# Where the forms of x and the sums of h are made: two layers of attention and squared-ReLU MLP, the MLP's first product by seven products

## The chip, the core and the metric

The kernel runs on one core of a Trainium2 chip. The metric is the time of one execution in device microseconds (us); each kernel is run several times and the median is given. The engines have the names of the profile: PE (matrix products; PEld is its loading of weights), DVE (vector engine), ACT (scalar engine), POOL (GpSimd) and SP, which here only issues transfers. Each engine executes its own instructions in the order in which they were written, and waits at an instruction until what it needs is there.

## The reference

Two layers, all in fp32, on x of 2048 rows and 640 columns: attention with 32 heads of 20, then an MLP with 1536 hidden columns.

```python
def _A_ref(x, wqkv, wo):
    q, k, v = ...                      # (x @ wqkv), 32 heads of 20
    scores = jnp.einsum("bhqd,bhkd->bhqk", q, k) * (Dh ** -0.5)
    p = _softmax(scores, axis=-1)
    o = jnp.einsum("bhqk,bhkd->bhqd", p, v)
    return o.transpose(0, 2, 1, 3).reshape(B, S, D) @ wo
def _B_ref(x, w1, b1, w2, b2):
    h = x @ w1 + b1
    h = jnp.where(h > 0, h, 0) ** 2
    return h @ w2 + b2
for _ in range(2):
    x = x + _A_ref(_layernorm(x), A_wqkv, A_wo)
    x = x + _B_ref(_layernorm(x), B_w1, B_b1, B_w2, B_b2)
```

## The kernel before

**Products in three terms.** PE multiplies in fp32r, a shorter form of fp32. Each operand is kept as two parts: `hi`, a cast to fp32r that ACT makes, and `lo = src - hi`, a subtraction, called lower part here. A product is three: hi hi, hi lo, lo hi (`THREE`).

**Stages of a layer.** Attention; then the *heads* (`add_heads`: the product with w_o, added to x, 32 half tiles of 128 x 320, four blocks of 512 rows in the order `HEADS = (1, 0, 2, 3)`, stored to `d_x`); then the MLP's first product (class `Up`) and its second product (class `Down`).

**First product.** It goes over four blocks of 512 rows in the order `UPS = (1, 2, 3, 0)`; a block has six units (`unit(qb, j, ...)`). The depth of 640 is five parts of 128. Four of them, as a 2 x 2 matrix of blocks, are multiplied by seven products instead of eight (Winograd's form of Strassen's scheme); the fifth is multiplied plainly. For this a unit needs *forms* of w_1 (A11, S2, S1, A22, S3, A12, S4; made once and kept in DRAM) and of x. Those of x are made anew for each block: `B11`, `B21`, `B22` are blocks of the normalised, transposed x, `T1_` to `T4_` are sums and differences of them, `LAST` is the fifth part and `LAST + 1` ("xd") a difference of it. A unit is 54 matmuls of 128 x 256 in the order A11, the product S4 of the unit before (its `tail`), S2, S1, A22, S3, A12, which use B11, B22, T2_, T1_, T4_, T3_ and B21. DVE adds the products out of the PSUM banks (L1498 `add(u1, bank[1], u0)`, L1523 to L1525 and L1546), ACT copies the first bank (L1493) and makes bias, ReLU and square. Units alternate between two sets of four banks, so PE can be a few products ahead of these sums and no more.

**Making the forms (class `Forms`).** For each half tile of rows (numbers 0 to 3 in a block; the second index of a form, 0 or 1, is the half of the rows):
- `load`: x from `d_x` to a tile (an SP transfer); `stats`: mean and variance (DVE L317, L318, then two small POOL instructions L320, L321); `turned`: normalise and transpose on DVE (L350, L355), store to `d_t`; `fetch`: four transfers that read it back across all partitions as `y`.
- `sums`, `third`, `fourth`: the sums T on POOL (`pool_lo`, L344).
- `split`, `plain`, `diff`: for a form, the cast on ACT (L460) and right behind it the lower part (L461) on DVE; only for T3_ and T4_ on POOL. `late` does this for B21, whose tile comes free with the block before.

**What sets the order.** `unit` calls `side()` seven times, 42 times in a block. Each call executes the entry of a table for that step: `Forms.PLACES[n]` for the next block and `Forms.PLACES[n - 42]` for the one after it (negative numbers are steps of the block before). The block that comes first is prepared beside the heads, by `BESIDE_HEADS`, one step for each of the 32 half tiles (`between`). SP issues all transfers in the order written, weights of w_1 and w_2 among them (`more`, `bring`).

**Sums of h for the second product.** `Down` uses seven products too (for all row blocks, but for the last block in layer 1). They need sums of four quarters of h. Before the change `tail` of a unit makes two of them on POOL when the unit's h is ready (L1551 and L1555, and a `pool_lo` behind each), stores one beside h (`d_h1`), and `Down.fetch` loads it again. `Down.make` makes the operands of a step of the second product two steps (`LEAD`) before its use.

Of the kernel before, what the change touches and what calls it, by code (L numbers as in the profile page):

```python
# [43 lines left out]
def tile_layers(  # L44
# [264 lines left out]
    d_h1 = dram.tile([NQB, NP, P, 2, P], F32, name="d_h1")  # L309
# [55 lines left out]
    class Forms:  # L365
# [3 lines left out]
            -9: [("load", 0), ("load", 2)],  # L369
            -3: [("stats", 0)],  # L370
            -1: [("stats", 2)],
            0: [("load", 1), ("load", 3)],
            3: [("turned", 0)],
            5: [("stats", 1)],
            9: [("turned", 2)],
            10: [("fetch", 0)],
            12: [("stats", 3)],
            16: [("turned", 1)],
            17: [("fetch", 2)],
            19: [("turned", 3)],  # L380
            21: [("sums", 0), ("third", 0)],
            23: [("split", B11, 0), ("fetch", 1)],
            24: [("split", B22, 0)],
            25: [("plain", 0)],
            26: [("split", T1_, 0)],
            27: [("split", T2_, 0), ("fetch", 3)],
            28: [("fourth", 0)],
            30: [("split", T3_, 0)],
            31: [("split", T4_, 0), ("diff", 0)],
            32: [("split", B11, 1)],  # L390
            33: [("split", B22, 1)],
            34: [("plain", 1)],
            35: [("sums", 1), ("third", 1)],
            37: [("split", T1_, 1)],
            38: [("split", T2_, 1)],
            40: [("split", T3_, 1), ("fourth", 1)],
            41: [("split", T4_, 1), ("diff", 1)],
        }
        BESIDE_HEADS = {
            10: [("load", 0), ("load", 2)],  # L400
            12: [("stats", 0)],
            13: [("stats", 2)],
            14: [("turned", 0)],
            15: [("turned", 2), ("load", 1), ("load", 3)],
            17: [("fetch", 0), ("stats", 1)],
            18: [("fetch", 2), ("stats", 3)],
            19: [("turned", 1)],
            20: [("turned", 3)],
            21: [("sums", 0)],
# [45 lines left out]
        def into(self, dst, src, i, lo=nc.vector.tensor_sub):  # L455
            hi_, lo_ = (
                dst[:, h, :, i * P : (i + 1) * P].rearrange("p k (a i) -> p k a i", a=4)
                for h in range(2)
            )
            nc.scalar.copy(hi_, src)  # L460
            lo(lo_, src, hi_.bitcast(F32))  # L461

# [1489 lines left out]
```

## Time and profile before

| what | value |
|---|---|
| median of 3 runs | 3566.66 us (3566.16 to 3568.74) |
| the profiled execution | 3570.83 us, span of its trace 3569.1 us |
| PE busy | 3511.4 us, 98% of the span |
| DVE, ACT, POOL busy | 2787.7, 2837.6 and 973.1 us (78%, 80%, 27%) |
| heads, layer 1 and 2 | about 1376 to 1444 and 3155 to 3224 us of the span |
| first product | 1449.2 to 1636.2 and 3227.9 to 3417.2 us |
| second product | 1636.2 to about 1747 and 3417.2 to about 3560 us |

The rest is attention. The profile gives for each engine when it was busy, and for each rest of an engine which instruction or transfer ended it. A busy PE can still be slow: the granted clock beside it says at which share of its full speed it ran. Line numbers in the rows are those of the kernel before (after the change the same lines stand up to 16 further on or 1 or 2 back).

### The profile page before, as it was taken

The numbers are of one execution on the slowest core, as the hardware profiler recorded it, in microseconds if no ns is written. First come the engines' busy times: TensorE is split into PE (matmuls) and PEld (weight loads), VectorE is DVE, ScalarE is ACT, GpSimd is POOL, SyncE is SP. The second block draws the span as 40 slices with busy tenths as digits, with TensorE's granted clock in tenths as the row PEclk, the third lists the DMA queues.
The fourth block names the chain that finished last, engine by engine and source line by source line (L and its number), as shares of the span: only waits on it lengthen the run. The fifth ranks groups of instructions, "written<-read, shape, count | busy, mean of one in ns | idle before, by whom it ended". The sixth has DMA issues, their size and how long they took to land.

```text
span 3569.1 us, 74141 instructions
## 1 busy us (share of the span) xinstructions
PE 3511.4 (98%) x26404; PEld 2167.9 (61%) x26404; DVE 2787.7 (78%) x5512; ACT 2837.6 (80%) x5038; POOL 973.1 (27%) x1213
## 2 busy tenths in 40 slices
PE   9999999999999999899999999999999999998899
PEld 8998333333333337889989973333333333378899
DVE  8999888888888872656869988888888888636567
ACT  5889999999999993354348899999999999934543
POOL 4430345444422121431143201212121212114410
PEclk9999999999999999999999999999999999999999
DMA  7666445444322137755666652222222121377554
GB/s 258 228 211 180 140 138 153 121 123 146 113 66 60 51 107 263 240 197 195 234 195 223 196 169 69 76 79 57 70 82 57 44 58 51 112 267 241 202 197 145
DMA packets 325056, 518.72 MB, mean 145 GB/s; under 512 B 74836, under 2 KB 149588, under 8 KB 324688
## 3 DMA queue, kind: packets, MB, share of 16 engines
q1 hardware_dynamic: 324160, 512.29, 45.8%
q8 instruction: 209, 3.42, 0.4%
q10 hardware_dynamic: 528, 1.70, 0.2%
q14 instruction: 159, 1.30, 0.1%
HBM read 331.14 MB, written 182.69 MB: 144 GB/s over the span
## 4 chain that ended last, share of the span: by engine, by line
PE 88%; DMA 4%; DVE 2%; issue 2%; ACT 2%; POOL 1%; SPq 1%; DVEq 0%; POOLq 0%; ACTq 0%
PE banks L946 27%; PE banks L931 18%; PE banks L837 17%; PE banks L1658 8%; PE banks L532 5%; PE banks L544 5%; PE banks L1463 4%; PE banks L512 2%; DMA y<-d_t 1%; SPq L80 1%; DVE xf L461 1%; DMA x<-d_x 1%; PE banks L527 1%; DMA d_t<-x 0%; PE banks L644 0%
## 5 line engine op out<-in xcount | busy, mean ns | idle before, releaser
L941 ACT ACTIVATE e<-banks 128x512 f32<-128x512 f32 (+1 forms) x3416 | 2035.3, 692 | 56.4 <-PE banks L931 20.9
L848 DVE TENSOR_REDUCE mx<-banks 128x1 f32<-128x512 f32 x2560 | 1619.5, 684 | 322.9 <-PE banks L837 271.6
L946 PE MATMUL banks<-e,vg 128*32 128x512 f32 x8192 | 1093.5, 605 | 2.3 <-ACT e L941 2.1
L837 PE MATMUL banks<-k,q 60*128 60x512 f32 x3360 | 1062.2, 411 | 0.7 <-DMA d_qk<-ev 0.7
L931 PE MATMUL banks<-q,k 62*128 62x512 f32 x4096 | 1049.6, 441 | 1.3 <-ACT v L608 0.6
L931 PEld LDWEIGHTS banks<-q,k 62*128 62x128 f32 x4096 | 514.9, 184 | 748.6 <-ACT e L941 441.4
L837 PEld LDWEIGHTS banks<-k,q 60*128 60x128 f32 x3360 | 569.8, 185 | 196.3 <-ACT e L941 63.6
L877 DVE CUSTOM_DVE_ANT_0 rl<-banks,rl 128x512 f32<-128x512 f32 x736 | 476.8, 688 | 31.4 <-PE banks L837 6.9
L870 ACT ACTIVATE rl<-banks 128x512 f32<-128x512 f32 x736 | 399.6, 602 | 56.8 <-PE banks L837 46.9
L946 PEld LDWEIGHTS banks<-e,vg 128*32 128x32 f32 x8192 | 162.2, 108 | 352.8 <-issue 268.6
L1463 PE MATMUL banks<-xf,w 128*128 128x256 f32 x2448 | 327.3, 293 | 46.5 <-DVE r L1524 16.3
L1463 PEld LDWEIGHTS banks<-xf,w 128*128 128x128 f32 x2448 | 313.4, 200 | 57.3 <-DVE r L1524 19.7
L544 PE MATMUL banks<-xnT,wqk 64*128 64x512 f32 x1080 | 327.6, 393 | 0.0
L532 PE MATMUL banks<-xnT,wqk 64*128 64x512 f32 x1080 | 327.1, 395 | 0.0
L990 POOL TENSOR_TENSOR few<-few,minus_t 128x16 f32<-128x16 f32 x62 | 179.9, 2901 | 243.8 <-DMA few<-d_s 243.7
L1001 POOL TENSOR_TENSOR o<-o 128x512 f32<-128x512 f32 x62 | 79.6, 1283 | 500.6 <-DMA o<-d_r 261.2
L341 POOL CAST mr<-nt 128x32 fp32r<-128x32 f32 x64 | 13.4, 209 | 742.2 <-DVE nt L903 742.2
L837 PE MATMUL banks<-kd,q 60*128 60x512 f32 x736 | 212.5, 398 | 0.8 <-ACT rl L870 0.6
L544 PEld LDWEIGHTS banks<-xnT,wqk 64*128 64x128 f32 x1080 | 202.1, 188 | 7.9
L532 PEld LDWEIGHTS banks<-xnT,wqk 64*128 64x128 f32 x1080 | 200.0, 187 | 11.1 <-issue 1.7
L532 PE MATMUL banks<-wv,xnT 64*128 64x320 f32 x960 | 193.5, 308 | 0.0
L544 PE MATMUL banks<-wv,xnT 64*128 64x320 f32 x960 | 190.4, 306 | 0.0
(150 smaller groups left out, 3543.1 us busy)
## 6 DMA issues: line engine op xcount, KB each, us to landing
q<-d_qk SPq DMA_DIRECT2D x876, 80.0 KB
d_qk<-ev SPq DMA_DIRECT2D x80, 512.0 KB
k<-d_qk SPq DMA_DIRECT2D x444, 80.0 KB
x<-d_x SPq DMA_DIRECT2D x96, 320.0 KB
w<-d_w SPq DMA_DIRECT2D x60, 480.0 KB
w<-d_w SPq DMA_DIRECT2D x48, 512.0 KB
d_o<-ot SPq DMA_DIRECT2D x248, 80.0 KB
ot<-d_o SPq DMA_DIRECT2D x38, 512.0 KB
```

What stands on the lines that cost most here:

```text
L532: top = nc.tensor.matmul(dst, a[:64], b[:64], start=start, stop=last)
L544: low = nc.tensor.matmul(dst, a, b, start=False, stop=last, skip_group_check=True)
L837: nc.tensor.matmul(dst, q_t[t][b : b + 60, p, sub * P : (sub + 1) * P], k_t[t // NQB, c][b : b + 60, p, :], start=True, stop=True,)
L848: nc.vector.tensor_reduce(maxima(t)[:, 2 * p + par, sub, c : c + 1], dst, axis=AX.X, op=ALU.max)
L870: nc.scalar.activation(r, dst, AF.Relu)
L877: nc.vector.tensor_tensor_reduce(out=r[par], in0=dst, in1=r[par], scale=1.0, scalar=LEAST, op0=ALU.add, op1=ALU.max, accum_out=maxima(t)[: ...
L931: nc.tensor.matmul(dst, k_t[t // NQB, kt // 4][b : b + 62, p, (kt % 4) * P : (kt % 4 + 1) * P], q_t[t][b : b + 62, p, :], start=True, stop ...
L941: nc.scalar.activation(dst, src, AF.Exp, scale=SCALE)
L946: nc.tensor.matmul(acc[32 * h : 32 * h + 32, :], v_t[t // NQB, kt // 8][:, kt % 8, 32 * h : 32 * h + 32], es[p][:, par, :], start=(kt == 0 ...
L990: nc.gpsimd.tensor_tensor(few, few, minus_t, op=ALU.pow)
L1463: nc.tensor.matmul(dst, w, v, start=n == 0 and not more, stop=n == len(todo) - 1, skip_group_check=more,)
L1658: nc.tensor.matmul(dst, a, b, start=first and not more, stop=last, skip_group_check=more)
```

## The change

The forms of x are made at other places and partly on another engine, and so are the sums of h:
- `cast` (ACT) and `low` (the lower part, now always on POOL) are separate entries of the tables, so that several casts can stand ahead of several lower parts. `both` does one and then the other. `late` makes both casts of B21 and then both lower parts, at step 0 of its block rather than 2.
- Both tables are new. Beside the heads the forms of the first block are made at steps 2 to 26 rather than 10 to 29, and from the tiles that `add_heads` has just made (`done`), so that these four tiles are not loaded from `d_x`. The first loads for the next block leave at step 26 of the heads rather than 29.
- The sums of h leave `Up`. `Down.sums` makes them on POOL in the second product, one step ahead of `make`; `d_h1` with its 30 stores and 30 loads is gone.
- The first three slots of w_1 are loaded in the last block of attention into tiles of k that are no longer used; beside the heads 12 slots are loaded instead of 14.

```diff
-            21: [("sums", 0), ("third", 0)],
-            23: [("split", B11, 0), ("fetch", 1)],
...
+            14: [("sums", 0), ("third", 0)],
+            15: [("cast", B11, 0), ("cast", B22, 0)],
+            16: [("turned", 3), ("low", B11, 0), ("low", B22, 0), ("cast", T2_, 0)],
...
-            24: [("split", T2_, 0), ("split", B21, 0)],
...
+            18: [("both", B11, 0), ("both", B22, 0), ("both", T2_, 0), ("both", T1_, 0)],
...
-    def into(self, dst, src, i, lo=nc.vector.tensor_sub):
...
-        nc.scalar.copy(hi_, src)
-        lo(lo_, src, hi_.bitcast(F32))
...
+        def cast(self, n, i):
+            self.part(n, i, lambda dst, src, i: nc.scalar.copy(self.at(dst, 0, i), src))
+        def low(self, n, i):
+            self.part(n, i, lambda dst, src, i: pool_lo(
+                self.at(dst, 1, i), src, self.at(dst, 0, i).bitcast(F32)
+            ))
...
+        for n, u in enumerate((6, 10, 14)):
+            def early(n=n):
...
+                del k_t[NG - 1, n]
+                kept.pop(((NG - 1) % 4, n))
+                w_1.load(n)
+            loads[t0 + 3, u] = early
...
+            if done is not None:
+                done[i] = x
...
-                if whole and pair:
-                    s = u0.rearrange("p (u c) -> p u c", u=2)
-                    nc.gpsimd.tensor_tensor(s, r[:, :, 2, :], r[:, :, 3, :], op=ALU.add)
-                    pool_lo(r[:, :, 2, :], r[:, :, 0, :], r[:, :, 2, :])
...
+        def sums(self, n):
+            un, grp, j = self.steps[n]
+            if grp:
+                return
+            raw = self.raw[un, j]
+            s = self.s[un, j] = xtile("s")[:, : 4 * P].rearrange("p (i f c) -> p f i c", f=2, i=2)
+            nc.gpsimd.tensor_tensor(s[:, 0], raw[:, :, 2, :], raw[:, :, 3, :], op=ALU.add)
+            pool_lo(raw[:, :, 2, :], raw[:, :, 0, :], raw[:, :, 2, :])
...
+                if n + self.LEAD + 1 < len(self.steps):
+                    self.sums(n + self.LEAD + 1)
...
-            made[UPS[1]].do(Forms.PLACES, {29: -9, 30: -3, 31: -1}.get(n))
-            more(n % 2 if n < 28 else 0)
+            made[UPS[1]].do(Forms.PLACES, {26: -12, 28: -8, 29: -5, 31: -1}.get(n))
+            more(n % 2 if n < 24 else 0)
...
-            add_heads(qb, x_a, x_m, xs, between)
+            add_heads(qb, x_a, x_m, xs, between, made[UPS[0]].x if n == 0 else None)
...
-                    if n == 2 and m:
+                    if n == 0 and m:
                         made[UPS[m]].late()
```

How the order of instructions moves is seen at three places of layer 1. A row is line, operation, output, inputs and size; the number behind a name tells tiles apart. DVE in the last unit of the first block, before: L1498, L1523 to L1525 and L1546 are the sums from the banks, `xf` and `xd` the lower parts of forms of the next block.

```order
L1498 TENSOR_TENSOR us_17129<-banks,us_17129 128x256
L461 TENSOR_TENSOR xf_17012<-t_17137,xf_17012 128x2x128
L461 TENSOR_TENSOR xf_17027<-t_17137,xf_17027 128x2x128
L317 BN_STATS bst_17182<-x_17109 128x6 x2
L318 BN_AGGR mv_17183<-bst_17182 128x2
L1523 TENSOR_TENSOR us_17129<-banks,us_17129 128x256
L1524 TENSOR_TENSOR r_17198<-banks,us_17129 128x2x128
L1525 TENSOR_TENSOR r_17198<-banks,us_17129 128x2x128
L461 TENSOR_TENSOR xd_17078<-t_17137,xd_17078 128x128
L317 BN_STATS bst_17223<-x_17111 128x6 x2
L318 BN_AGGR mv_17224<-bst_17223 128x2
L1546 TENSOR_TENSOR r_17198<-banks,us_17129 128x2x128
```

The same unit after the change; the sums are now L1514, L1538 to L1540 and L1561.

```order
L1514 TENSOR_TENSOR us_17121<-banks,us_17121 128x256
L316 BN_STATS bst_17153<-x_17066 128x6 x2
L317 BN_AGGR mv_17154<-bst_17153 128x2
L1538 TENSOR_TENSOR us_17121<-banks,us_17121 128x256
L1539 TENSOR_TENSOR r_17189<-banks,us_17121 128x2x128
L1540 TENSOR_TENSOR r_17189<-banks,us_17121 128x2x128
L349 TENSOR_SCALAR y_17206<-x_17064,mv_17115 128x5x4x32
L354 STREAM_TRANSPOSE x_17064<-y_17206 128x640
L1561 TENSOR_TENSOR r_17189<-banks,us_17121 128x2x128
```

Three lower parts are gone from between the sums; statistics have moved up, and normalising and transposing a tile of the block after the next (L349, L354) stands ahead of the last sum.

DVE at the end of the heads, before: L1443 is the add of a half tile, L317 and L318 are statistics of the first two tiles of the second block, L1498 is the first sum of the first product.

```order
L1443 TENSOR_TENSOR x_16375<-banks,x_16375 128x320
L461 TENSOR_TENSOR xd_16547<-t_16522,xd_16547 128x128
L1443 TENSOR_TENSOR x_16419<-banks,x_16419 128x320
L317 BN_STATS bst_16645<-x_16624 128x6 x2
L318 BN_AGGR mv_16646<-bst_16645 128x2
L1443 TENSOR_TENSOR x_16419<-banks,x_16419 128x320
L317 BN_STATS bst_16668<-x_16626 128x6 x2
L318 BN_AGGR mv_16669<-bst_16668 128x2
L1498 TENSOR_TENSOR us_16676<-banks,us_16676 128x256
```

After the change, with L1457 for the add:

```order
L1457 TENSOR_TENSOR x_16410<-banks,x_16410 128x320
L316 BN_STATS bst_16605<-x_16568 128x6 x2
L317 BN_AGGR mv_16606<-bst_16605 128x2
L1457 TENSOR_TENSOR x_16410<-banks,x_16410 128x320
L316 BN_STATS bst_16628<-x_16570 128x6 x2
L317 BN_AGGR mv_16629<-bst_16628 128x2
L1457 TENSOR_TENSOR x_16461<-banks,x_16461 128x320 x2
L349 TENSOR_SCALAR y_16668<-x_16568,mv_16606 128x5x4x32
L354 STREAM_TRANSPOSE x_16568<-y_16668 128x640
L1514 TENSOR_TENSOR us_16673<-banks,us_16673 128x256
```

The statistics have moved ahead of three and two adds, and behind the last add now stand L349 and L354, the first tile's normalising and transposing.

POOL at the end of the first block, before: `xf` are lower parts of T3_ and T4_, L1551 and the row behind it the sums of h, `t` and `y` the sums of forms, `mv` the end of statistics.

```order
L1551 TENSOR_TENSOR us_17034<-r_17101 128x256
L344 TENSOR_TENSOR r_17101<-r_17101 128x2x128
L320 TENSOR_TENSOR mv_17183<-mv_17183,eps_t 128x1
L321 TENSOR_TENSOR mv_17183<-mv_17183,half_t 128x1
L344 TENSOR_TENSOR xf_17066<-y_16911,xf_17066 128x2x128
L344 TENSOR_TENSOR t_17137<-y_16871,t_17137 128x256
L344 TENSOR_TENSOR xf_17075<-t_17137,xf_17075 128x2x128
L320 TENSOR_TENSOR mv_17224<-mv_17224,eps_t 128x1
L321 TENSOR_TENSOR mv_17224<-mv_17224,half_t 128x1
L1551 TENSOR_TENSOR us_17129<-r_17198 128x256
L344 TENSOR_TENSOR r_17198<-r_17198 128x2x128
```

POOL at the same place after the change:

```order
L319 TENSOR_TENSOR mv_17115<-mv_17115,eps_t 128x1
L320 TENSOR_TENSOR mv_17115<-mv_17115,half_t 128x1
L319 TENSOR_TENSOR mv_17154<-mv_17154,eps_t 128x1
L320 TENSOR_TENSOR mv_17154<-mv_17154,half_t 128x1
L343 TENSOR_TENSOR xf_16968<-t_17036,xf_16968 128x2x128
L343 TENSOR_TENSOR xd_16908<-t_17036,xd_16908 128x128
L343 TENSOR_TENSOR xf_16905<-y_16823,xf_16905 128x128
L343 TENSOR_TENSOR xf_16905<-y_16876,xf_16905 128x128
L343 TENSOR_TENSOR xf_16867<-y_16876,xf_16867 128x2x128
L343 TENSOR_TENSOR xf_17218<-y_16668,xf_17218 128x2x128
L343 TENSOR_TENSOR xf_17218<-y_16823,xf_17218 128x2x128
```

The sums of h are gone, and a run of lower parts stands there, all of the second half of the rows and then the late B21 (the last two rows).

More of the change, by code (lines that the diff above doesn't have):

```diff
@@ L1482, in flush, with unit @@
             self.store()
-        def unit(self, qb, j, x, whole, free, keep=None):
+        def unit(self, qb, j, x, free, keep=None):
             side = self.side
@@ L1866, in layer @@
         w_1.drop()
+        down.sums(2)
         early = [None] * 60
```

175 lines of the change are left out of this document (80 added, 95 removed).

## The prediction

> **What bounds the kernel now.** I read four views in this order: busy time by stage, the timeline of PE where one block of rows gives way to the next, the timeline of DVE at the same places, and the groups of instructions by line. First the stages. Columns: stretch and its length, busy time of PE, PEld, DVE, ACT and POOL (with instructions), granted clock, DMA share, GB/s. The six rows are heads, first product and second product of layer 1, then the same of layer 2.
>
> ```profile
> 1376.00:1444.00 68.00, 68.00 (x465) 67.87 (x463) 36.09 (x67) 6.72 (x19) 11.53 (x20) 1.00 0.93 313
> 1449.20:1636.20 187.00, 168.68 (x1296) 163.92 (x1297) 106.97 (x228) 92.07 (x209) 66.41 (x109) 0.95 0.65 216
> 1636.20:1747.00 110.80, 110.80 (x758) 110.80 (x758) 91.20 (x184) 42.27 (x82) 7.16 (x12) 1.00 0.58 196
> 3155.00:3224.00 69.00, 69.00 (x467) 68.29 (x465) 37.10 (x68) 6.70 (x19) 12.00 (x21) 1.00 0.92 308
> 3227.90:3417.20 189.30, 170.06 (x1296) 164.46 (x1297) 108.52 (x228) 91.95 (x209) 75.96 (x121) 0.95 0.65 218
> 3417.20:3560.00 142.80, 142.80 (x977) 142.80 (x976) 112.42 (x224) 53.81 (x106) 3.40 (x4) 1.00 0.49 161
> ```
>
> Heads and second product have a PE that never rests at clock 1.00: nothing is to be had there. The first product is PE work too (1296 matmuls in each layer), but PE rests some 18 us in it and its clock is 0.95. Next PE at the switch from the first block of rows to the second. A unit is 54 matmuls and has one group "xd" (3 matmuls), so the distance of two xd rows is the time of a unit. In brackets stands the idle time before a row and what ended it.
>
> ```profile
> 1473.07 0.52 PE L1463 MATMUL banks<-xd,w 128*128 128x256 f32 x3
> ...
> 1478.88 4.99 PE L1463 MATMUL banks<-xf,w 128*128 128x256 f32 x27 [2.42 <-DVE r L1524]
> 1483.71 0.52 PE L1463 MATMUL banks<-xd,w 128*128 128x256 f32 x3
> ...
> 1490.19 0.52 PE L1463 MATMUL banks<-xd,w 128*128 128x256 f32 x3
> 1491.79 3.14 PE L1463 MATMUL banks<-xf,w 128*128 128x256 f32 x24 [1.07 <-DVE us L1498]
> 1496.42 2.78 PE L1463 MATMUL banks<-xf,w 128*128 128x256 f32 x21 [1.49 <-DVE r L1524]
> 1500.39 0.38 PE L1463 MATMUL banks<-xf,w 128*128 128x256 f32 x1 [1.20 <-ACT xf L460]
> 1501.20 0.86 PE L1463 MATMUL banks<-xf,w 128*128 128x256 f32 x5 [0.42 <-POOL xf L344]
> 1501.90 0.52 PE L1463 MATMUL banks<-xd,w 128*128 128x256 f32 x3
> 1503.01 1.86 PE L1463 MATMUL banks<-xf,w 128*128 128x256 f32 x10 [0.59 <-DVE us L1498]
> ...
> 1511.66 0.52 PE L1463 MATMUL banks<-xd,w 128*128 128x256 f32 x3
> ...
> 1539.16 0.52 PE L1463 MATMUL banks<-xd,w 128*128 128x256 f32 x3
> ```
>
> From 1483.71 to 1490.19 a unit takes 6.48 us (0.120 us for a matmul); 24 units would take 155.5 us, and the stages take 187.0 and 189.3. Where is the excess? The four units from 1473.07 to 1511.66 take 38.59 us instead of 25.92: 12.67 lost at one switch, and a layer has three. The four units from there to 1539.16 take 27.50, so only 1.58 goes where nothing special happens. The clock of 0.95 belongs to the same thing: the matmuls after a rest run longer (27 in 4.99 us at 1478.88, where 27 in a row are 3.24).
>
> The releasers are named DVE: sums of banks (L1498, L1523, L1524), which free banks for PE. DVE works in order, so I look at what stands ahead of these sums.
>
> ```profile
> 1488.85 2.22 DVE L461 TENSOR_TENSOR xf<-y,xf 128x256 fp32r<-128x256 f32 x3 [2.12 <-ACT xf L460]
> ...
> 1492.93 1.65 DVE L461 TENSOR_TENSOR xf<-t,xf 128x256 fp32r<-128x256 f32 x2 [1.20 <-ACT xf L460]
> ...
> 1500.64 0.65 DVE L461 TENSOR_TENSOR xd<-t,xd 128x128 fp32r<-128x128 f32 x1 [3.95 <-ACT xd L460]
> ```
>
> Ahead of them stand lower parts (L461, `src - hi`) that wait for their cast on ACT, up to 3.95 us with DVE idle and PE's sums queued behind. DVE is not full here (106.97 of 187.0 us); it is held. At 1500.39 PE also waits 1.20 us for a cast itself, of the late form B21.
>
> The last place is the end of the heads in layer 1 and 2, PE and DVE:
>
> ```profile
> 1447.60 0.89 DVE L317 BATCH_NORM_STATS2 bst<-x 128x6 f32<-128x320 f32 x2 [1.32 <-DMA x<-d_x]
> ...
> 1448.64 0.44 DVE L1443 TENSOR_TENSOR x<-banks,x 128x320 f32<-128x320 f32 x1
> ```
> ```profile
> 1449.18 4.61 PE L1463 MATMUL banks<-xf,w 128*128 128x256 f32 x24 [5.05 <-issue]
> 3227.87 4.53 PE L1463 MATMUL banks<-xf,w 128*128 128x256 f32 x24 [3.88 <-issue]
> ```
>
> The first product wants the bank that the last add of the heads (L1443) frees. That add stands behind statistics of rows whose load lands at 1447.6, so PE rests 5.05 and 3.88 us.
>
> **The change part by part.** The groups from which the prices come (busy time, mean ns of one, then idle time before them):
>
> ```profile
> L461 DVE TENSOR_TENSOR xf<-y,xf 128x256 fp32r<-128x256 f32 (+1 forms) x80 | 51.0, 675 | 35.1 <-ACT xf L460 33.3 <-DMA w<-d_w 1.5
> L461 DVE TENSOR_TENSOR xf<-t,xf 128x256 fp32r<-128x256 f32 x32 | 18.8, 601 | 19.2 <-ACT xf L460 19.2
> L461 DVE TENSOR_TENSOR xd<-t,xd 128x128 fp32r<-128x128 f32 x16 | 7.1, 446 | 37.9 <-ACT xd L460 19.8 <-POOL us L1551 8.8 <-ACT us L1493 4.3
> L344 POOL TENSOR_TENSOR xf<-y,xf 128x256 fp32r<-128x256 f32 x16 | 12.6, 789 | 19.1 <-ACT xf L460 19.1
> L1551 POOL TENSOR_TENSOR us<-r 128x256 f32<-128x256 f32 x30 | 22.1, 738 | 31.8 <-ACT r L1521 31.8
> L1555 POOL TENSOR_TENSOR s<-r 128x128 f32<-128x128 f32 x24 | 12.7, 528 | 60.3 <-ACT r L1521 60.3
> ```
>
> *Lower parts to Pool.* DVE loses 128 instructions of 76.9 us and, what counts, their waits of 92.2 us (35.1 + 19.2 + 37.9). Its sums in the first product then wait for PE alone. Pool takes on 16 lower parts for each of 8 blocks: 10 of 128x256 at 0.789 and 6 of 128x128, whose nearest row is 0.528: 11.1 us. Six of the eight blocks prepare the one behind them. If all of Pool's time in the two stages stood in these six, they held (66.41 + 75.96) / 6 = 23.7 us each; with 11.1 more and (22.1 + 12.7) / 8 = 4.4 less for the sums of h that leave, Pool has at most 30.4 us of work in a block's 38.9. Since the second sum of each pair leaves too, I expect some 25. Where it waits for a cast, only statistics and other forms stand behind it, nothing that frees a bank.
>
> The Trainium skill speaks against this part: GPSIMD Engine Reference, section 4.1, Engine selection, wants elementwise additions on VectorE, as GPSIMD takes about twice as long for two inputs. The trace agrees on the price of one (0.41 us on DVE alone at 1443.02 below, 0.789 here). By that rule the part would cost some 11.1 - 9.6 = 1.5 us a block, 12 us in all, if these instructions were on the path; they are beside it here, and the sum has nothing for it.
>
> *New places.* Most casts stand earlier by 3 to 10 of the 42 steps (0.926 us each; those of B22 and of the last fifth for the second half of the rows later by 3 or 4), and a lower part one or two steps behind its cast. Casts are as many as before, on an ACT busy 92.07 of 187.0. An ACT held by a late load would hold the copy of PE's first bank (L1493); from a unit's first product to the product that needs it stand 30 matmuls, 3.6 us, less copy and sum 0.9: a margin of 2.7 us, to which the steps until the next copy are added. I cost it at nothing in the middle value. B21 is made at step 0 rather than 2 of its block: 1.85 us earlier against the 1.20 + 0.42 that PE waited.
>
> *Rows beside the heads.* The block that comes first takes its rows where the heads made them: four loads fewer a layer, forms finished by steps 18 to 26 rather than 22 to 29. Loads of the next block leave at step 26 rather than 29, some 6 us sooner, and the adds no longer stand behind casts or lower parts. The wait of 5.05 and 3.88 becomes the add and its hand-overs, 0.7 us by the rows at 1448.64 (0.44) and 1449.18 (0.54 later).
>
> *Sums of h.* They leave the first product with 60 small transfers, and Pool does two of 128x256 (0.738) for each of 42 steps of the second product, one step ahead of their use: 6 x 0.738 = 4.4 us for every 17.8 us of PE (142.80 / 8). Pool was idle there (3.40 of 142.80). DVE is the neighbour: (142.80 - 112.42) / 8 = 3.8 us idle in each such stretch. How much Pool slows DVE:
>
> ```profile
> 1441.74 0.96 DVE L461 TENSOR_TENSOR xf<-t,xf 128x256 fp32r<-128x256 f32 x1
> ...
> 1443.02 0.41 DVE L461 TENSOR_TENSOR xf<-t,xf 128x256 fp32r<-128x256 f32 x1
> ```
> ```profile
> 1441.64 0.78 POOL L344 TENSOR_TENSOR y<-y 128x256 f32<-128x256 f32 x1
> ```
>
> Beside a Pool instruction the same lower part takes 0.96 instead of 0.41, a loss of 0.55 at most for each Pool instruction: 6 x 0.55 = 3.3 us, under the 3.8 idle. Cost: nothing, but the cover is thin. The Trainium skill, SBUF — State Buffer, section Who interferes with whom, says that a DVE instruction with two SBUF inputs and a GpSimd read lock each other out of a shared port for a whole instruction. By that the loss could be Pool's whole 4.4 us, 0.6 over the idle, 8 us over the 14 stretches; the trace shows 0.55 of 0.78, so I keep to the row.
>
> *Weights.* Three slots of w_1 load in the last block of attention, into tiles no longer read, and the heads load 12 rather than 14. DMA share in the heads is 0.93, so fewer transfers only help; PE's order is the same row by row.
>
> *What stays.* The last unit's own wait:
>
> ```profile
> 1630.60 0.52 PE L1463 MATMUL banks<-xd,w 128*128 128x256 f32 x3
> 1632.76 3.65 PE L1463 MATMUL banks<-xf,w 128*128 128x256 f32 x27 [1.64 <-DVE us L1498]
> 1636.25 1.04 PE L1658 MATMUL banks<-w,hb 128*128 128x320 f32 x6
> ```
>
> From the xd row to the second product are 30 matmuls, 3.60 us; they take 5.65. These 2.05 us come from the first operands of the second product, whose lower parts stay on DVE.
>
> *Sum.* Layer 1: 187.0 - 155.5 - 2.05 = 29.4; layer 2: 189.3 - 155.5 - 2.05 = 31.8; gaps 5.05 + 3.88 - 1.4 = 7.5. Together 68.7. Off this I take 4 us for small waits that stay or are new, from the 1.58 that four plain units lose already (two or three such stretches in each layer: 0 to 8). That is 65 us. The profiled execution took 3570.83 with a span of 3569.1, so 3506 and 3504; the median of the runs is 4.2 lower, 3566.66 - 65 = 3502.
>
> **The rivals.** *Part of the waits comes back on ACT.* Loads of transposed rows are slow:
>
> ```profile
> 1468.43 2.26 SPq L80 DMA_DIRECT2D y<-d_t  x4
> ...
> 1475.56 0.74 POOL L344 TENSOR_TENSOR t<-y,y 128x256 f32<-128x256 f32 x1 [7.67 <-DMA d_t<-x]
> ```
>
> Four transfers issued from 1468.43 are read at 1475.56, 7.1 us later. The new places leave 4 or 5 steps, 3.7 to 4.6 us, between the last such load and its sums, so ACT may stand 2.5 to 3.4 us, and Pool 1.5 us more, at two points of a block. Against it: the next copy stands some five steps behind. If the margin fails, each of six switches loses 2 to 5 us: 12 to 30 back, 3514 to 3532, middle 3520.
>
> *DVE becomes the bound of the second product.* If the thin cover fails: 0.6 us x 14 = 8, so 3510.
>
> *Slower.* Pool falls so far behind that PE waits for lower parts at each switch. The decisive point: Pool's work of a block exceeds its 38.9 us by more than the 11 us that a switch loses now, 50 us, which needs Pool instructions nearly twice as long as these rows. At 55 us a block six blocks would give 6 x 16 = 96 against 65: 3598. None of the rows shows Pool so slow, even beside DVE.
>
> *The change moves nothing on PE*, because the late rows and not DVE's order set the switch: then 3566. Against it: PE is released by sums that had no need of those rows.
>
> **How the numbers follow.** My forecast 0.70, its own range 3495 (no small waits, and the 4 us of the last units gone too) to 3509. Waits back on ACT 0.18, second product 0.06, nothing moved 0.03, slower 0.03. To leave out no more than 2 in 10, the range goes from 3493 up to 3530. The bound between a change and none is 0.2%, 7 us; faster 0.94, within 0.03, slower 0.03.
>
> **What would show it.** Right: xd rows 6.48 us apart across each switch; no lower part of x on DVE in the first product; the first matmul of that stage 1 us or less behind the heads; granted clock 1.00 there; Pool near 24 us a block; PE full in the second product. Wrong: matmuls released by ACT's copy of the first bank or by Pool's lower parts, or DVE full in the second product.

## The result and the profile after

The changed kernel takes 3509.28 us (3508.60 to 3511.64), the kernel before 3567.42 in the runs beside it: a ratio of 0.9838, interval 0.9821 to 0.9855. It gains 58 us; the forecast was 3502, in a range of 3493 to 3530. The two profiled executions differ by 61.6 us in span (3569.1 and 3507.5).

Busy time by stage of the kernel after, with the columns of the prediction (heads, first product, second product of layer 1, then of layer 2):

```profile
1376.00:1444.00 68.00, 67.89 (x463) 67.62 (x462) 31.44 (x60) 6.91 (x21) 23.35 (x42) 1.00 0.91 305
1444.50:1607.20 162.70, 158.02 (x1297) 157.33 (x1298) 80.21 (x177) 91.64 (x209) 67.33 (x114) 0.99 0.70 236
1607.20:1718.00 110.80, 109.82 (x749) 109.47 (x748) 96.60 (x182) 42.12 (x82) 32.16 (x40) 1.00 0.52 177
3125.00:3193.00 68.00, 68.00 (x465) 68.00 (x464) 31.23 (x59) 6.92 (x21) 23.26 (x42) 1.00 0.90 309
3193.90:3354.10 160.20, 156.23 (x1296) 155.76 (x1297) 79.85 (x177) 91.68 (x209) 67.36 (x114) 1.00 0.70 240
3354.10:3497.00 142.90, 141.92 (x968) 141.56 (x967) 120.19 (x223) 53.37 (x106) 38.11 (x44) 1.00 0.43 144
```

The first product takes 162.7 and 160.2 us instead of 187.0 and 189.3, at clock 0.99 and 1.00 instead of 0.95. PE now rests 4.7 and 4.0 us in it. In the second product DVE is busier (120.19 us where it was 112.42, in windows of almost one length), POOL too, and PE rests 0.98 us. PE at the start of both first products and at the first switch of layer 1:

```profile
1444.52 3.11 PE L1479 MATMUL banks<-xf,w 128*128 128x256 f32 x24 [0.63 <-issue]
...
1480.74 0.52 PE L1479 MATMUL banks<-xd,w 128*128 128x256 f32 x3
1483.92 7.88 PE L1479 MATMUL banks<-xf,w 128*128 128x256 f32 x51 [2.66 <-DVE us L1514]
1491.64 0.52 PE L1479 MATMUL banks<-xd,w 128*128 128x256 f32 x3
1498.12 0.52 PE L1479 MATMUL banks<-xd,w 128*128 128x256 f32 x3
...
1603.69 3.65 PE L1479 MATMUL banks<-xf,w 128*128 128x256 f32 x27 [1.38 <-DVE us L1514]
1618.89 1.15 PE L1662 MATMUL banks<-w,hc 128*128 128x320 f32 x6 [0.98 <-ACT u L1753]
```
```profile
3193.94 3.11 PE L1479 MATMUL banks<-xf,w 128*128 128x256 f32 x24 [0.63 <-issue]
...
3232.35 6.37 PE L1479 MATMUL banks<-xf,w 128*128 128x256 f32 x51 [2.55 <-DVE us L1514]
```

The gaps behind the heads are 0.63 us instead of 5.05 and 3.88, and xd rows are 6.48 us apart from 1491.64 to the last unit. Of the three switches between blocks only the first of each layer still costs time. From 1480.74 to 1491.64 are 10.90 us instead of 6.48: 2.66 of the lost 4.4 us are the wait, and the rest are slower matmuls behind it (51 in 7.88 us, where the row at 3232.35 has 51 in 6.37). At that place DVE, POOL and ACT:

```profile
1481.60 0.89 DVE L316 BATCH_NORM_STATS2 bst<-x 128x6 f32<-128x320 f32 x2 [4.48 <-DMA x<-d_x]
...
1482.64 0.37 DVE L1561 TENSOR_TENSOR r<-banks,us 128x256 f32<-128x256 f32 x1
1483.44 0.42 DVE L1514 TENSOR_TENSOR us<-banks,us 128x256 f32<-128x256 f32 x1 [0.43 <-issue]
```
```profile
1478.75 0.74 POOL L343 TENSOR_TENSOR t<-y,y 128x256 f32<-128x256 f32 x1 [7.65 <-DMA w<-d_w]
```
```profile
1480.33 0.71 ACT L479 CAST xf<-t 128x256 fp32r<-128x256 f32 x2 [6.10 <-POOL t L343]
...
1482.99 0.36 ACT L1509 COPY us<-banks 128x256 f32<-128x256 f32 x1
```

Two chains arrive late together. DVE stands 4.48 us at statistics whose load has not landed, and the sum L1514 stands behind them. POOL waits for transposed rows, ACT's cast waits for POOL, and ACT's copy (L1509), which L1514 needs as well, stands behind the cast. The POOL row names `w<-d_w`, a transfer that SP issues behind the rows; the instruction itself reads only `y`, and at the same place of layer 2 (3227.17) it waits 7.58 us with `y<-d_t` as the releaser.

### The profile page after: what moved, and what is told of

Its sections match the earlier page's. It is cut to its first block, busy times and chain, and to the rows that moved or that the text cites. A ratio compares the mean times of both kernels' runs of the same rounds, so it can differ in the third digit from the quotient of the medians.

```text
span 3507.5 us, 74034 instructions
## 1 busy us (share of the span) xinstructions
PE 3485.3 (99%) x26404; PEld 2150.9 (61%) x26404; DVE 2733.5 (78%) x5384; ACT 2835.8 (81%) x5038; POOL 1046.2 (30%) x1317
## 3 DMA queue, kind: packets, MB, share of 16 engines
q14 instruction: 158, 1.29, 0.1%
## 4 chain that ended last, share of the span: by engine, by line
PE 57%; DMA 1%; DVE 1%; ACT 1%; issue 0%; POOL 0%; SPq 0%; DVEq 0%; POOLq 0%; ACTq 0%
PE banks L951 14%; PE banks L936 9%; PE banks L842 9%; PE banks L1662 8%; PE banks L1479 7%; PE banks L517 4%; PE banks L537 3%; PE banks L549 2%; DMA y<-d_t 1%; PE banks L532 0%; DMA x<-d_x 0%; PE banks L649 0%; ACT e L946 0%; SPq L80 0%; DMA w<-d_w 0%
## 5 line engine op out<-in xcount | busy, mean ns | idle before, releaser
L853 DVE TENSOR_REDUCE mx<-banks 128x1 f32<-128x512 f32 x2560 | 1619.9, 684 | 321.9 <-PE banks L842 272.6
L1479 PE MATMUL banks<-xf,w 128*128 128x256 f32 x2448 | 304.5, 284 | 9.9 <-DVE us L1514 8.0
L1479 PEld LDWEIGHTS banks<-xf,w 128*128 128x128 f32 x2448 | 298.9, 193 | 11.5 <-DVE us L1514 8.8
```

The lines of the kernel that those rows point to most:

```text
L853: nc.vector.tensor_reduce(maxima(t)[:, 2 * p + par, sub, c : c + 1], dst, axis=AX.X, op=ALU.max)
L1479: nc.tensor.matmul(dst, w, v, start=n == 0 and not more, stop=n == len(todo) - 1, skip_group_check=more,)
```

## The experiments

Gaps are both waits behind the heads; the other columns are the length of the first product in the profile, from its first matmul to the first of the second product. The ratio is to the kernel before, in runs on the same chip. The lengths are those of one profiled execution. The changed kernel, e4 and e11, whose times agree, have 322.8, 323.5 and 321.9 us in both layers together, and up to 3.2 us between them in one layer; so differences of a few us in this column are weak evidence (an estimate from these three).

| kernel | median us | ratio, interval | gaps | layer 1 | layer 2 |
|---|---|---|---|---|---|
| before | 3567 to 3571 | 1 | 8.93 | 187.1 | 189.4 |
| after | 3509.3 | 0.9838 (0.9821 to 0.9855) | 1.26 | 162.7 | 160.2 |
| e1 lower parts on DVE | 3515.1 | 0.9845 (0.9831 to 0.9860) | 1.26 | 163.0 | 164.2 |
| e7 e1, casts beside them | 3517.5 | 0.9852 (0.9839 to 0.9866) | 1.26 | 165.5 | 165.8 |
| e12 e7, sums of h in Up | 3522.2 | 0.9862 (0.9845 to 0.9878) | 1.26 | 168.8 | 169.9 |
| e10 before, new places | 3534.6 | 0.9897 (0.9881 to 0.9914) | 11.88 | 169.0 | 172.1 |
| e2 before, lower parts on POOL | 3551.8 | 0.9945 (0.9930 to 0.9960) | 12.47 | 178.3 | 179.0 |
| e3 after, sums of h in Up | 3511.1 | 0.9834 (0.9819 to 0.9849) | 1.26 | 164.4 | 162.6 |
| e4 after, loads at 29 | 3508.0 | 0.9824 (0.9807 to 0.9840) | 1.26 | 163.4 | 160.2 |
| e11 after, B21 at step 2 | 3510.4 | 0.9832 (0.9817 to 0.9846) | 1.26 | 160.1 | 161.8 |
| e5 after, statistics later | 3517.1 | 0.9853 (0.9840 to 0.9867) | 1.26 | 162.5 | 166.0 |
| e8 e5, operands at 37 | 3511.4 | 0.9837 (0.9823 to 0.9850) | 1.26 | 160.0 | 163.7 |
| e6 after, loads earlier | 3510.0 | 0.9834 (0.9820 to 0.9847) | 1.26 | 160.3 | 159.2 |
| e9 e6, rows earlier, operands at 37 | 3499.8 | 0.9804 (0.9789 to 0.9819) | 1.26 | 156.8 | 156.1 |

**e1: the engine undone.** Lower parts go back to DVE, at the new places (those of T3_ and T4_ stay on POOL, where they were before the change):

```diff
+            sub = pool_lo if n in (T3_, T4_) else nc.vector.tensor_sub
-            self.part(n, i, lambda dst, src, i: pool_lo(
+            self.part(n, i, lambda dst, src, i: sub(
```

> The changed kernel (3509) with the lower parts back on DVE (those of T3_ and T4_ stay on POOL), at the new places. Theory A, the engine decides: DVE is in order, and any lower part on it that waits for a cast holds PE's sums; the waits at the switches come back, first product 175 to 187 us in a layer, time 3530 to 3560. Theory B, the places decide: with casts one or two steps ahead of the lower parts DVE seldom waits for them, first product 160 to 165 us, time 3507 to 3518.

3515.1 us, theory B. Groups by line of e1:

```profile
L1480 PE MATMUL banks<-xf,w 128*128 128x256 f32 x2448 | 306.1, 284 | 12.9 <-DVE r L1540 8.7 <-DVE us L1515 2.8 <-issue 1.3
L483 DVE TENSOR_TENSOR xf<-y,xf 128x256 fp32r<-128x256 f32 (+1 forms) x80 | 32.7, 447 | 11.9 <-ACT xf L479 10.4 <-DMA y<-d_t 1.5
L483 DVE TENSOR_TENSOR xf<-t,xf 128x256 fp32r<-128x256 f32 x32 | 15.4, 520 | 14.3 <-ACT xf L479 14.3
```

PE waits 12.9 us in all, where it was 46.5 before and is 9.9 after. The same lower parts on the same engine now wait 11.9 + 14.3 us, nearly all of it for casts, instead of 35.1 + 19.2.

**e2: the engine alone.** The kernel before, all lower parts on POOL at the old places:

```diff
-        def into(self, dst, src, i, lo=nc.vector.tensor_sub):
+        def into(self, dst, src, i, lo=pool_lo):
-            self.into(self.res[n], src, i, pool_lo if n in (T3_, T4_) else nc.vector.tensor_sub)
+            self.into(self.res[n], src, i)
```

> The kernel before (3567) with only the engine changed: all lower parts on POOL, at the old places. Theory A, the engine decides: the sums on DVE no longer stand behind casts, and what stays is B21's late cast and lower part (about 1.6 us and a cold clock at each of six switches) and the gap behind the heads (8.9 us): 3520 to 3535. Theory B, the places decide: casts on ACT are as late as before and POOL's lower parts follow them late, so PE waits for POOL instead of DVE: 3555 to 3575.

3551.8 us, between the two theories: 19 to 20 us of the 58. PE's waits have changed their names, as theory B said, but are shorter. PE of e2, the gap behind the heads of layer 1, a wait for weights and a switch:

```profile
1450.68 5.40 PE L1463 MATMUL banks<-xf,w 128*128 128x256 f32 x24 [6.57 <-issue]
...
1491.83 0.62 PE L1463 MATMUL banks<-xd,w 128*128 128x256 f32 x3 [3.18 <-DMA w<-d_w]
...
1505.84 5.18 PE L1463 MATMUL banks<-xf,w 128*128 128x256 f32 x41 [1.66 <-POOL xf L344]
```

Two losses here have nothing to do with the sums on DVE. PE waits for weights of w_1, 3.18 us in layer 1 and 3.43 in layer 2, where the kernel before has no such wait, and both gaps behind the heads are longer (12.47 us together instead of 8.93). So 19 to 20 us is what the engine gains net of some 10 us of new waits. No run shows what it gains without them.

**e7: distance or hour.** e1 with each cast right ahead of its lower part (`cast` does nothing, `low` does both):

```diff
...
+            def pair(dst, src, i):
+                nc.scalar.copy(self.at(dst, 0, i), src)
+                lo(self.at(dst, 1, i), src, self.at(dst, 0, i).bitcast(F32))
+            self.part(n, i, pair)
```

> The kernel of e1 (lower parts on DVE, new places, 3515) with each cast right ahead of its lower part, at the place of the lower part. Theory B1, the distance decides: DVE again meets each lower part before ACT has made its cast, holds the sums, and the gain goes: 3535 to 3560. Theory B2, the earlier hour decides (forms begun when their rows have landed, the late B21 two steps earlier, heads finished in time): 3512 to 3522.

3517.5 us, theory B2: the earlier hour does it (the steps at which rows are fetched and forms made), and the distance between a cast and its lower part adds little. Groups of e7:

```profile
L1483 PE MATMUL banks<-xf,w 128*128 128x256 f32 x2448 | 307.8, 285 | 15.3 <-DVE r L1543 11.3 <-DVE us L1518 2.8 <-issue 1.3
L486 DVE TENSOR_TENSOR xf<-y,xf 128x256 fp32r<-128x256 f32 (+1 forms) x80 | 31.6, 431 | 23.6 <-ACT xf L485 22.8 <-DMA y<-d_t 0.8
L486 DVE TENSOR_TENSOR xf<-t,xf 128x256 fp32r<-128x256 f32 x32 | 15.5, 524 | 17.2 <-ACT xf L485 17.2
```

DVE does wait more for casts than in e1 (23.6 + 17.2 against 11.9 + 14.3), but these waits end while PE still has free banks: PE's own waits grow by 2.4 us only, from 12.9 to 15.3.

**e10: the hour alone.** The kernel before with the whole new table for the first product (loads, rows and sums of forms at the new steps, `split` at the step of `low`) and B21 at step 0. Forms beside the heads and sums of h stay as they were. The end of the heads differs a little: the first loads still leave at step 29, but the first tile is now normalised and transposed at step 31. From the edit:

```diff
-            41: [("split", T4_, 1), ("diff", 1)],
+            38: [("split", T4_, 1), ("diff", 1)],
...
-                    if n == 2 and m:
+                    if n == 0 and m:
```

> The kernel before (3567) with the new places in the first product alone: each cast right ahead of its lower part at the lower part's new step, lower parts on DVE as before, B21 at step 0; forms beside the heads and sums of h as before. Theory B2, the earlier hour decides: the switches lose 2 to 4 us instead of 11 to 13, some 45 to 52 us of the gain is there: 3515 to 3525. Rival: the hour alone does little while POOL still carries the sums of h between its other work and the heads' end is as before: 3540 to 3560.

3534.6 us, between the two theories: better than the rival and short of what B2 said. Some 37 of the 58 us are there, although the gaps behind the heads are 3 us longer than before (11.88 instead of 8.93). Its group in PE still waits 29.5 us, 11.9 of it behind the heads:

```profile
L1462 PE MATMUL banks<-xf,w 128*128 128x256 f32 x2448 | 313.1, 288 | 29.5 <-DVE r L1523 13.6 <-issue 11.9 <-DVE us L1497 4.0
```

**e12: sums of h, with the lower parts on DVE.** e7 with the sums made in `Up.tail` again, stored and loaded as before.

> The kernel of e7 (new places, casts beside their lower parts, lower parts on DVE, 3517) with the sums of h made in the first product again. Theory K, a ring of waits: POOL waits at these sums for ACT's squares, with the sums of forms behind it; ACT waits for those, DVE for ACT's casts, and ACT's squares for DVE; while the lower parts are on DVE the sums of h cost what they didn't cost in e3: 3522 to 3530. Theory L: at the new places there is room for them in any case, and the 17 us between the places alone (e10) and e7 come from the heads and what is prepared there: 3515 to 3520.

3522.2 us, at the border of theory K, and too close to e7 for the times alone: the intervals of the two ratios overlap, and the four runs of e12 lie between 3516 and 3524, the profiled one being the slowest. By length the first product takes 168.8 and 169.9 us against 165.5 and 165.8 in e7, 7.4 us more in all, and 2.4 less than in e10. Read so, about 7 us of the way from e10 to e7 are the sums of h and 11 the gaps behind the heads; these executions suggest it and do not prove it.

**e3: sums of h, with the lower parts on POOL.** The changed kernel with the sums in `Up.tail`.

> The changed kernel with the sums of h made and stored in the first product again, as before. Theory A: the sums of h moved no time to speak of by leaving; POOL goes from some 25 to 34 us of 38.9 in a block and still keeps up; the wait of 0.98 us in the second product of each layer goes: 3505 to 3513. Theory C: POOL is free for the lower parts only because the sums have left; in the first product PE waits for POOL's lower parts at the switches, 2 to 5 us each: 3521 to 3540.

3511.1 us, theory A. The first product is 4.2 us longer by the table; the wait of 0.98 us in the second product is gone from its timeline, and the time is that of the changed kernel within the intervals.

**e4: the gap behind the heads.**

```diff
-            made[UPS[1]].do(Forms.PLACES, {26: -12, 28: -8, 29: -5, 31: -1}.get(n))
+            made[UPS[1]].do(Forms.PLACES, {29: -12, 30: -8, 31: -5}.get(n))
+            if n == 31:
+                made[UPS[1]].do(Forms.PLACES, -1)
```

> The changed kernel with the first two loads for the second block at step 29 of the heads rather than 26, and statistics at 30 and 31. Theory A: the gap behind the heads (now 0.63 us) was the wait of the last add behind these statistics; it comes back to 3 to 5 us a layer, 6 to 9 in all: 3515 to 3519. Theory D: the gap came from casts and lower parts that filled DVE at the end of the heads, and these are gone: 3508 to 3511.

3508.0 us, theory D. DVE of e4 at the end of the heads:

```profile
1442.15 0.49 DVE L1457 TENSOR_TENSOR x<-banks,x 128x320 f32<-128x320 f32 x1 [1.76 <-PE banks L517]
1442.56 0.88 DVE L316 BATCH_NORM_STATS2 bst<-x 128x6 f32<-128x320 f32 x2
...
1444.29 0.49 DVE L1457 TENSOR_TENSOR x<-banks,x 128x320 f32<-128x320 f32 x1 [0.62 <-PE banks L517]
```

The statistics stand where they stood before, and find their rows landed. The load comes from the same step 29, but SP issues it at 1436.38 us; it left at 1439.71 before the change and leaves at 1443.42 in e10. So DVE and the transfers no longer run late. e10, which has the later loads and the old forms beside the heads, keeps the gap (7.87 and 4.01 us). It is not the engine: e1 and e7, with lower parts on DVE, have no gap either. Whether the earlier forms do it or the four loads fewer, no run shows.

**e11: B21 at step 2.**

```diff
-                    if n == 0 and m:
+                    if n == 2 and m:
                         made[UPS[m]].late()
```

> The changed kernel with B21 made at step 2 of its block rather than 0. Theory: its cast waits for nothing but its place, so PE waits for it again as before (1.20 + 0.42 us at each of six switches, more on POOL, whose two lower parts follow both casts): 10 to 20 us more, 3519 to 3530. Rival: that wait was the outcome of ACT being late for other reasons; 3508 to 3513.

3510.4 us, the rival: no wait of PE for B21 is in its timeline. So the step of B21 was not what PE waited for before; that ACT came late to its cast for other reasons is what is left.

**e5, e6, e8, e9: the first switch.** e5 puts statistics at -2 and -1 and normalising at 2 and 3; e8 is e5 with `36: down.make` at 37; e6 only moves two loads (those beside the heads stay at step 26); e9 adds to e6 that the transposed rows are fetched earlier and that the first operands of the second product are made at step 37:

```diff
-            -12: [("load", 0), ("load", 2)],
+            -18: [("load", 0), ("load", 2)],
...
-            17: [("cast", T1_, 0), ("low", T2_, 0), ("low", T1_, 0)],
+            17: [("cast", T1_, 0), ("low", T2_, 0), ("low", T1_, 0), ("fetch", 1)],
...
-            19: [("low", LAST, 0), ("low", LAST + 1, 0), ("fetch", 1)],
+            19: [("low", LAST, 0), ("low", LAST + 1, 0)],
+            20: [("fetch", 3)],
...
-            23: [("low", T3_, 0), ("low", T4_, 0), ("end", 0), ("fetch", 3)],
+            23: [("low", T3_, 0), ("low", T4_, 0), ("end", 0)],
...
-                36: down.make, 40: down.make}
+                37: down.make, 40: down.make}
```

> The changed kernel (3509) with the statistics of the next block's first two tiles at steps -2 and -1 rather than -8 and -5, normalising and transposing at 2 and 3 rather than -1 and 2. Theory E: the one wait left at the first switch of each layer (2.66 and 2.55 us, 4.4 and 2.8 with the cold clock) is DVE held by the first of these statistics for a load that lands 6.6 us after its issue; later statistics find it landed and the wait is gone: 3501 to 3504. Theory F: something else is late there too (the transposed rows' loads now follow closer on their stores, forms of the third block come late), and the time stays at 3508 to 3512.

> The changed kernel with the loads of the next block's first two tiles six steps (5.6 us) earlier, at step -18 rather than -12, and nothing else moved. Theory E: they land before the statistics want them, and the wait at the first switch goes: 3501 to 3504. Theory G: a tile for them isn't free that early, or the transfers of the first block (DMA is busy with w_1) are merely late in a row, so the load lands as late as before and holds other transfers in the queue: 3508 to 3515.

> The kernel of e5 with the first operands of the second product made at step 37 rather than 36, behind the sum L1514 instead of ahead of it. Theory: the wait of 1.38 us in each layer's last unit is that sum standing behind the lower parts of these operands; it goes, some 1.5 to 2 us a layer, 3 to 4 below e5: 3497 to 3501. Rival: the operands are then late for the second product's first matmuls, and the same time is lost there: no gain on e5.

e5 is slower than the changed kernel, 3517.1 us, and slower than either theory had it: the wait at the first switch stays (1.86 and 2.87 us), a new one stands two units ahead of it (1.39 and 1.18), and layer 2 has a third (1.29). Two units ahead the rows that were normalised later hold ACT, and its copy comes late; ACT of e5:

```profile
1463.80 0.41 ACT L478 CAST xf<-y 128x256 fp32r<-128x256 f32 x1 [2.80 <-DMA y<-d_t]
1465.58 0.71 ACT L478 CAST xf<-t 128x256 fp32r<-128x256 f32 x2 [1.38 <-POOL t L343]
...
1468.55 0.36 ACT L1508 COPY us<-banks 128x256 f32<-128x256 f32 x1
```

e6 is no faster by its time, 3510.0 us, in the range of theory G, though its load lands earlier, as theory E had it: the statistics wait 1.17 us instead of 4.48. DVE of e6 at the first switch:

```profile
1478.68 0.89 DVE L316 BATCH_NORM_STATS2 bst<-x 128x6 f32<-128x320 f32 x2 [1.17 <-DMA x<-d_x]
...
1482.86 0.42 DVE L1514 TENSOR_TENSOR us<-banks,us 128x256 f32<-128x256 f32 x1 [2.77 <-ACT us L1509]
```

With the first chain out of the way the second one shows: L1514 now waits for ACT's copy, which stands behind the cast that waits for POOL. PE waits 1.30 us there instead of 2.66. e8 comes to 3511.4 us, outside the 3497 to 3501 expected, which had counted on e5 being fast. Against e5 it gains 5.7 us: it takes the wait of the last unit away (no such row is left in its timeline), and the first product of both layers together is 4.8 us shorter than e5's.

> The kernel of e6 with the transposed rows of the second half fetched at steps 17 and 20 rather than 19 and 23, and the first operands of the second product made at step 37 rather than 36. Theory H: two things are late together at the first switch, the statistics' load (4.48 us of DVE) and, behind it, the fetched rows, for which POOL and through it ACT stand 6.1 us; with both earlier the wait goes (2.66 us and its cold clock), and the last unit's 1.38 too: 8 to 11 below the changed kernel, 3498 to 3502. Rival: the transfers of the first block are short of bandwidth (DMA share 0.93 there), an earlier issue lands no earlier, and only the last units gain: 3505 to 3508.

3499.8 us (3498.95 to 3503.47), theory H. Its group in PE:

```profile
L1480 PE MATMUL banks<-xf,w 128*128 128x256 f32 x2448 | 302.7, 283 | 1.8 <-issue 1.3 <-DVE r L1540 0.4
```

The first product takes 156.8 and 156.1 us, against 155.5 for 24 units without a wait. In layer 1 SP issues the rows 2.9 us earlier than in e6 (1467.87 instead of 1470.79), POOL starts its sums 2.0 us earlier (1476.17 instead of 1478.16), and PE no longer waits there. This version is faster than both kernels: its ratio is 0.9804, up to 0.9819, and that of the changed kernel 0.9838, from 0.9821. Of its three edits only the earlier loads were also run alone.

## Why the prediction was right, and where it was not

**The terms.** The first product gave 24.4 us in layer 1 and 29.3 in layer 2 (foretold 29.4 and 31.8), the gaps 7.7 (7.5). The term for small waits was mis-sized: 4 us stood in the sum and some 9 were lost (68.7 without any small wait, 59.4 measured). The first switches alone cost 4.4 and 2.8, and the second product lost 0.98 twice. The 59.4 us are most of the 61.6 between the spans; the other 2 lie outside these stages, the larger part between the second product of layer 1 and the heads of layer 2, and what makes them is open. The forecast of 65 is 3.4 above the spans' difference. Another 3.5 lie between spans and medians: the profiled execution of before was 3.4 us above the median of its runs now, that of after (3509.26) stands at its median. So 3509.28 lies inside the stated range, but at the very edge of the 3495 to 3509 that the forecast gave itself without the rivals. The reading that 12.67 us are lost at one switch and a layer has three was also too even: in layer 1 the third switch lost 4.7, as its xd rows show.

**The first rival was partly true.** One half of the wait that stayed is what it priced: transposed rows that land late, POOL and ACT held, the copy late. The other half, statistics waiting for their load, no rival had. The first rival's wait was given to all six switches; it occurs at the first of each layer. The rows of after show why. SP's issues in the first and the second block, POOL's first use, and the two blocks' windows (DMA share and GB/s at the end):

```profile
1471.09 1.76 SPq L80 DMA_DIRECT2D y<-d_t  x4
```
```profile
1508.41 3.20 SPq L80 DMA_DIRECT2D y<-d_t  x4
```
```profile
1513.74 0.74 POOL L343 TENSOR_TENSOR t<-y,y 128x256 f32<-128x256 f32 x1 [1.18 <-DVE r L1539]
```
```profile
1444.50:1482.00 37.50, 36.12 (x297) 35.73 (x297) 18.85 (x39) 17.35 (x39) 13.41 (x23) 1.00 0.93 296
1483.90:1521.00 37.10, 37.08 (x296) 37.08 (x297) 21.56 (x47) 22.14 (x52) 22.76 (x40) 0.95 0.59 192
```

In the first block, while w_1 is still loading, rows issued at 1471.09 are read at 1478.75, 7.7 us later, at a DMA share of 0.93. In the second, at 0.59, 5.3 us pass, and POOL's releaser there is no transfer, so the rows had landed sooner than that. In the third, the same rows take 4.3 us (1547.31 to 1551.63), and POOL waits for no transfer either. A wait of POOL for the rows of the other half, 2.74 us at 1542.01, costs PE nothing there. The prediction read the 7.1 us of before, from the first block, as the price for all blocks.

**The cause was put in the wrong place.** The prediction gave the gain to lower parts leaving DVE, and saw in the new places of the first product, B21 apart, a risk that it costed at nothing, and no gain. The runs turn this round. The places alone give 37 us (e10), the engine alone 19 to 20 (e2, with 10 us of new waits in it). With all else changed, the engine is worth 4.4 us of first product (e1 to after) and the distance between cast and lower part 4.1 (e7 to e1). Both figures come from single executions; by the times, whose intervals overlap, they are 2 to 3 us each. The terms do not add. The reading that fits is that either change breaks the same chain, in which DVE waits for ACT's casts, ACT for POOL's sums of forms, and POOL's queue for ACT's squares. The first and the last link are in the groups of the prediction (L461, and L1551 with [31.8 <-ACT r L1521]); ACT of before shows the middle one:

```profile
1499.94 0.40 ACT L460 CAST xf<-t 128x256 fp32r<-128x256 f32 x1 [1.15 <-POOL t L344]
```

That the chain closes on itself is argued from these names and not shown: no run takes one link alone away, and e12 against e3 (sums of h cost 7.4 us of first product with lower parts on DVE, 4.2 with them on POOL) differs by little more than the lengths scatter. The sum came out because it asked what is left when the waits are gone, not which edit takes them. In that respect the right figure was luck: the same sum would have stood if only the other half of the change had mattered.

**The gap behind the heads** went as foretold, 0.63 against 0.7, but not by the earlier loads: e4 has the later ones and no gap. The row with [1.32 <-DMA x<-d_x] named a load that was itself issued late, 3.3 us later than in e4 from the same step. The prediction's other reason, adds that no longer stand behind casts or lower parts, fits e4.

**B21.** Step 0 gained nothing over step 2 (e11).

**The second product.** POOL takes 38.11 us there in layer 2, at instructions longer than the 0.738 us that they were priced at. Groups of after:

```profile
L1612 POOL TENSOR_TENSOR s<-r 128x256 f32<-128x256 f32 x42 | 38.2, 908 | 214.9 <-DMA r<-d_h 94.1 <-ACT r L1536 72.5 <-DVE hc L329 23.8
L343 POOL TENSOR_TENSOR r<-r 128x256 f32<-128x256 f32 x42 | 35.0, 832 | 3.3
L343 POOL TENSOR_TENSOR xf<-t,xf 128x256 fp32r<-128x256 f32 x48 | 34.9, 744 | 5.9 <-ACT xf L479 5.9
```

DVE gained 7.8 us of busy time in layer 2, of some 30 that it had free, about 1 us in each of the eight stretches where up to 3.3 were foretold. The cover held except at the stage's start, where POOL makes eight sums in a row and PE waits 0.98 us for ACT, which stands behind a cast that waits for DVE. With the sums of h in the first product (e3) this wait is gone.

**POOL's load.** 22.76 us in a window of 37.10 is 23.9 for a block, against some 25 foretold. The rule of the Trainium skill (GPSIMD Engine Reference, section 4.1, Engine selection) holds roughly for the price: 0.744 us on POOL against 0.41 on DVE, 1.8 times as long. The prediction's 1.5 us a block "by that rule" was worked from the rows; a factor of two on the 9.6 us of a block would have made it 9.6. Neither decided, as no wait of PE in the first product names POOL.

## What to carry to other kernels

Where engines wait for one another in order, look at when an input is ready and how far ahead its step stands before moving work to another engine: here the new places alone brought 37 us and the new engine alone 19 to 20. A chain of waits has one price, and several edits can each earn it; test them alone before crediting one. A transfer's time from issue to use must be read in the block where it is used, with the DMA share beside it.

## What the hardware showed

DVE and POOL take turns at instructions that read two inputs from SBUF. DVE and POOL of after at the start of the second product, and DVE behind it:

```profile
1614.19 0.96 DVE L1649 TENSOR_TENSOR s<-r,s 128x256 f32<-128x256 f32 x1
1615.08 1.23 DVE L329 TENSOR_TENSOR hc<-r,hc 128x512 fp32r<-128x512 f32 x1
1616.23 0.96 DVE L329 TENSOR_TENSOR hd<-s,hd 128x256 fp32r<-128x256 f32 x1
...
1618.00 0.68 DVE L329 TENSOR_TENSOR hc<-r,hc 128x512 fp32r<-128x512 f32 x1
1618.60 0.41 DVE L329 TENSOR_TENSOR hd<-s,hd 128x256 fp32r<-128x256 f32 x1
```
```profile
1609.04 1.36 POOL L1612 TENSOR_TENSOR s<-r 128x256 f32<-128x256 f32 x1 [14.07 <-ACT r L1536]
...
1613.68 1.19 POOL L1612 TENSOR_TENSOR s<-r 128x256 f32<-128x256 f32 x1
1614.95 0.81 POOL L343 TENSOR_TENSOR r<-r 128x256 f32<-128x256 f32 x1
1615.72 1.19 POOL L1612 TENSOR_TENSOR s<-r 128x256 f32<-128x256 f32 x1
1616.99 0.80 POOL L343 TENSOR_TENSOR r<-r 128x256 f32<-128x256 f32 x1
```

While POOL works, until 1617.8, each of these DVE instructions takes 0.55 us more, whatever its size (0.96 for 0.41, 1.23 for 0.68), and POOL's take up to 1.36 instead of 0.74. The ends show why (start plus length). They alternate: POOL 1614.87, DVE 1615.15, POOL 1615.76, DVE 1616.31, POOL 1616.91, DVE 1617.19, POOL 1617.79. Each POOL instruction ends 0.60 or 0.61 us behind the DVE instruction before it, and each DVE instruction 0.28 (128x256) or 0.55 us (128x512) behind the POOL instruction before it. That is one instruction after the other, and not two that share a rate. The Trainium skill, SBUF — State Buffer, section Who interferes with whom, calls the port pair that the two engines share an exclusive lock; the ends agree with it. DVE's sums out of the banks, with one input from SBUF, keep their 0.41 to 0.43 us beside POOL (1506 to 1530 of the same trace). The prediction had the 0.55 from one row and priced only DVE's loss, not POOL's.
